# Keys' exponential features in a first stage: fronts two tiles ahead of the sums, sums of features alone for two tiles at a time

## The chip, the cores and the metric

The kernel runs on one core of a Trainium2 chip. The core has TensorE (matrix products, PE in the profile), VectorE (DVE), ScalarE (ACT), GpSimd (POOL) and SyncE (SP, which issues the transfers here). Each works through its own queue in order. The metric is the device time of one execution in microseconds, as the median of several runs.

## The reference

A linear attention feeds two expert layers. The change lies in the attention's keys:

```python
def phi(x):
    proj = np.einsum('bhsd,df->bhsf', x, w_phi)
    proj = proj - np.max(np.abs(proj), axis=-1, keepdims=True)
    return np.concatenate([np.exp(proj), np.exp(-proj)], axis=-1)
q_p, k_p = (phi(q), phi(k))
kv = np.einsum('bhsf,bhsd->bhfd', k_p, v)
z = np.sum(k_p, axis=2)
num = np.einsum('bhsf,bhfd->bhsd', q_p, kv)
den = np.einsum('bhsf,bhf->bhs', q_p, z)[..., None] + 1e-06
return (num / den).astype(np.float32)
```

There are 4 batches, 8 heads, 576 positions, heads of 64 and 128 features, so 256 with both signs. Its result goes, scaled by a root mean square, through a gated layer (512 to 1536 and back), and through a second layer of 8 experts with soft slots.

## The kernel before

**Stages.** Stage one makes the sums kv and z of all four batches, attends the first block of 384 queries, and converts nine of the 18 pieces of the gated layer's weights (each by two passes on ACT, L127 and L129, two on DVE, L137 and L139, a rounding on ACT, L102, and a difference on POOL, L105). Stage two is the gated layer over six blocks (L804, and L829 to L831), with the further queries and weights worked in between. Stage three is the second layer. Stage two begins on TensorE with the first L804.

**A tile of keys.** The 2304 positions make 18 tiles of 128. A tile's *front* is: eight matmuls of the keys with the features (L394, into two buffers P, one for each half hf of the heads), DVE's largest value and its subtraction (L398, L402, into `pr`, three buffers), and ACT's two exponentials (L415, L416, into a buffer `kp` for each half, four in all). A tile's *sums* are eight matmuls of values with features (`kv_of`, L439: 64 columns of the array each, into the accumulators kacc0 for hf 0 and kacc1 for hf 1) and eight of ones with features (`z_of`, L448: 32 columns each, into kacc2). The keys come by L385 (four buffers `raw`), the values by L411 (three).

**Batches.** A batch is 4.5 tiles. Tiles 4 and 13 hold the end of one batch and the start of the next, and their sums are made in two parts; batch 1 ends with tile 8. Where a batch ends, `Evac` copies the accumulators out: kacc0 and kacc2 on ACT (L463), kacc1 on DVE (L461). The accumulators have one buffer each, so the next batch's first sum waits for that copy. The copies are then turned on TensorE (L476) and laid out by L485 and L487.

**The loop over tiles (L519)** issues in turn i: the loads, the front of tile i + 1 up to DVE's subtraction, the sums of tile i, then the exponentials of tile i + 1, with pieces of weight conversion, of turning and of the first block's queries (L322, L325, L326, L337, L339, L206, L214, L216 to L232) between the halves. Ahead of the loop stands the front of tile 0. The order in which each engine gets its instructions is not just this order: a scheduler puts an instruction that it takes for ready ahead of one that it takes for waiting. So runs of matmuls of one line are cut by others.

Of the kernel before, what the change touches and what calls it, by code (L numbers as in the profile page):

```python
# [7 lines left out]
F32 = mybir.dt.float32  # L8
# [8 lines left out]
NB, NH, SEQ, HD, DF = 4, 8, 576, 64, 128  # L17
# [3 lines left out]
TILES = NT // 128  # L21
# [19 lines left out]
def batch_parts(i):  # L41

    t0, parts = i * 128, []
    r = 0
    while r < 128:
        b = (t0 + r) // SEQ
        end = min(128, (b + 1) * SEQ - t0)
        parts.append((b, r, end))
        r = end
    return parts  # L50
# [14 lines left out]
def tile_kernel(ctx: ExitStack, tc: tile.TileContext, q2T, qT, kT, v, wbd, wg, wv, wo, rmsg, phi, w1, w2, consts, out):  # L65
# [3 lines left out]
    def pool(stack, name, space=None, bufs=1, side="left"):  # L69
        kw = {} if space is None else {"space": space}  # L70
        if space is None:
            kw["side"] = side
        if space is not DRAM:
            kw["reuse_waits"] = "tile"
        return stack.enter_context(tc.tile_pool(name=name, bufs=bufs, **kw))
# [73 lines left out]
    def conv_load(sp, bufs, *pools):  # L149

        key = next(conv_at, None)
        if key is not None:
            c = Conv(sp, pools[pieces.index(key) % len(pools)], key, bufs)
            c.load()
            loaded.append(c)

    def conv_scale():
        if loaded:
            convs.append(loaded.pop(0))
            convs[-1].scale()  # L160

    def conv_join():
        if convs:
            convs[-1].join()
            if convs[-1].n == 2:
                joined.append(convs.pop())

    def conv_parts():
        if joined:
            joined.pop(0).parts()  # L170
# [85 lines left out]
    class Reduced(Q):  # L256
# [25 lines left out]
        def exps(self, h):  # L282
            e = self.e[h]
            DVE.tensor_tensor(out=e[:, 1], in0=e[:, 1], in1=e[:, 0], op=ALU.subtract)
            ACT.activation(out=e[:, 0], in_=e[:, 1], func=AF.Exp)
            ACT.activation(out=e[:, 1], in_=e[:, 1], func=AF.Exp, scale=-1.0)
# [83 lines left out]
    with ExitStack() as pk:  # L370
        kx = pool(pk, "kx")
        sp = pool(pk, "spk")
        psk = pool(pk, "psk", PSUM)
        acc = {}

        class Front:

# [30 lines left out]
        class K(Front):  # L408
# [2 lines left out]
                SP.dma_start(out=self.vt, in_=v[self.i].rearrange("p (h d) -> p h d", h=NH))  # L411

            def exps(self, hf):
                kp = sp.tile([128, 4, 2, DF], F32, tag="kp", name="kp", bufs=4)
                ACT.activation(out=kp[:, :, 0], in_=self.pr[hf], func=AF.Exp)  # L415
                ACT.activation(out=kp[:, :, 1], in_=self.pr[hf], func=AF.Exp, scale=-1.0)  # L416
                self.e[hf] = kp

            def kv(self, part):

                for f in (self.kv_of, self.z_of):
                    for hf in range(2):
                        f(hf, part)

            def ends(self, part):
                b, r0, r1 = part
# [66 lines left out]
        ks = [K(sp, psk, kT, i, kb if i else dict(kb, P=("misc", 3))) for i in range(TILES)]  # L493
# [13 lines left out]
        for _ in range(2):  # L507
            conv_load(sp, KCONV, sp)
        conv_scale()
        ks[0].project()  # L510
        for hf in range(2):
            ks[0].shift(hf)
            ks[0].exps(hf)
        fillers = []
        q0 = Turned(sp, psk, 0, {"misc": 3, "raw": 2, "pr": 3, "e": 2})
        qsteps = q0.steps(TURNED0[0:4], TURNED0[4:8], TURNED0[8:])
        qsteps = [[f for m, f in qsteps if m == n] for n in range(2 * TILES)]
        q0.begin()
        for i in range(TILES):  # L519
            k, kn = ks[i], ks[i + 1] if i + 1 < TILES else None  # L520
            if i + 3 < TILES:
                ks[i + 3].load()
            if i + 2 < TILES:
                ks[i + 2].load_v()
            if i % 2 and i // 2 + 2 < NPRE:
                conv_load(sp, KCONV, sp)
            parts = batch_parts(i)
            b = parts[0][0]
            ends = i * 128 + parts[0][2] == (b + 1) * SEQ

            def finish():
                ev = Evac(b)
                fillers.extend([lambda n=n: ev.turn(n) for n in range(3)])

            if len(parts) > 1:
                k.kv(parts[0])
                finish()
            if kn:
                kn.project()
                kn.shift(0)  # L540
                kn.largest(1)
                conv_join()
                kn.less(1)
            k.kv(parts[-1])
            for hf in range(2):
                if kn:
                    kn.exps(hf)
                if hf == 0 and i % 2:
                    conv_parts()
                    conv_scale()  # L550
                if fillers:
                    fillers.pop(0)()
                for f in qsteps[2 * i + hf]:
                    f()
            if ends and len(parts) == 1:
                finish()
# [47 lines left out]
    with ExitStack() as p2:  # L604
# [5 lines left out]
        sp = pool(tctx, "conv")  # L610
# [233 lines left out]
        for blk in range(NBLK):  # L844
            acc = [ps.tile([128, DM], F32, tag=f"acc{i}", name=f"acc{i}", bufs=1) for i in range(TPB)]
            qsteps, qnext = qnext or [], None
            if blk == 1:
# [6 lines left out]
                sp = pool(pctx, "post", side="right")  # L854
            if blk == NBLK - 1:
# [5 lines left out]
                sp = pool(pctx, "post", side="right")  # L861
# [62 lines left out]
    with ExitStack() as p3:  # L924
        sp = pool(p3, "sp3")
# [145 lines left out]
```

## Time and profile before

| what | value |
| --- | --- |
| time, median of 3 runs | 745.16 us (744.03 to 750.23) |
| profiled execution, its time | 744.73 us |
| profiled execution, its span | 742.9 us |
| TensorE busy, whole span | 713.5 us, 96% |
| VectorE, ScalarE busy | 428.1 us, 371.6 us |
| first L804 on TensorE (end of stage one) | 134.23 us |

The busy time of an engine is the time in which an instruction of its was at work; matmuls overlap a little in their records, so that a row's own duration is somewhat longer than the step to the next row. A matmul of this type leaves two records, so "x16" in a row is eight matmuls. In a timeline, a bracket behind a row gives the idle time ahead of it and what ended it.

### The profile page before, as it was taken

The numbers are of one execution on the slowest core, as the hardware profiler recorded it, in microseconds if no ns is written. First come the engines' busy times: TensorE is split into PE (matmuls) and PEld (weight loads), VectorE is DVE, ScalarE is ACT, GpSimd is POOL, SyncE is SP. The second block draws the span as 40 slices with busy tenths as digits, with TensorE's granted clock in tenths as the row PEclk, the third lists the DMA queues.
The fourth block names the chain that finished last, engine by engine and source line by source line (L and its number), as shares of the span: only waits on it lengthen the run. The fifth ranks groups of instructions, "written<-read, shape, count | busy, mean of one in ns | idle before, by whom it ended". The sixth has DMA issues, their size and how long they took to land.

```text
span 742.9 us, 12354 instructions
## 1 busy us (share of the span) xinstructions
PE 713.5 (96%) x4919; PEld 575.1 (77%) x4919; DVE 428.1 (58%) x808; ACT 371.6 (50%) x805; POOL 108.3 (15%) x60
## 2 busy tenths in 40 slices
PE   6999898999899999999999999999999999999894
PEld 4555554888789888898888988889888899988343
DVE  5888956687756646555565555655556453323313
ACT  6689855588644465334654346543465431211103
POOL 0222210135200211012110121101211010000100
PEclk9999999999999999999999999999999999999998
DMA  9674211545010100101000010000100237657898
GB/s 325 225 243 182 72 44 45 187 158 208 8 61 23 33 22 23 49 0 33 22 23 20 1 33 22 23 19 1 33 1 2 65 120 275 228 199 288 318 362 285
DMA packets 25146, 79.47 MB, mean 107 GB/s; under 512 B 2688, under 2 KB 13376, under 8 KB 18688
## 3 DMA queue, kind: packets, MB, share of 16 engines
q1 hardware_dynamic: 24864, 77.79, 30.0%
q10 hardware_dynamic: 224, 0.88, 0.4%
q8 instruction: 39, 0.64, 0.3%
q14 instruction: 19, 0.16, 0.1%
HBM read 71.99 MB, written 6.67 MB: 106 GB/s over the span
## 4 chain that ended last, share of the span: by engine, by line
PE 76%; ACT 10%; DVE 6%; issue 2%; DMA 2%; POOL 1%; SPq 0%; DVEq 0%; ACTq 0%; POOLq 0%
PE pv L804 18%; PE pg L804 17%; PE acc L829 6%; PE acc L830 6%; PE acc L831 6%; PE num L206 4%; PE kacc L439 3%; PE den L214 2%; PE y L943 2%; ACT e L224 2%; PE kacc L448 2%; PE y L959 2%; DVE wt L137 1%; DMA wraw<-in_wg_dram 1%; ACT wt L127 1%
## 5 line engine op out<-in xcount | busy, mean ns | idle before, releaser
L804 PE MATMUL pv<-xnh,wv 128*128 128x384 f32 x576 | 151.6, 344 | 0.0
L804 PE MATMUL pg<-xnh,wg 128*128 128x384 f32 x576 | 150.2, 342 | 1.3 <-DVE t L812 1.0
L804 PEld LDWEIGHTS pg<-xnh,wg 128*128 128x128 f32 x576 | 104.7, 188 | 7.2 <-DVE t L812 1.5
L804 PEld LDWEIGHTS pv<-xnh,wv 128*128 128x128 f32 x576 | 103.2, 188 | 7.0 <-issue 6.7
L804 PE MATMUL pv<-xnl,wv 128*128 128x384 f32 x288 | 97.7, 339 | 0.0
L804 PE MATMUL pg<-xnl,wg 128*128 128x384 f32 x288 | 97.5, 338 | 0.0
L829 PE MATMUL acc<-wo,hh 128*128 128x512 f32 x216 | 88.6, 410 | 0.0
L280 POOL PARTITION_ALL_REDUCE qe<-qe x32 | 50.0, 1563 | 262.7 <-ACT qe L279 243.0
L830 PE MATMUL acc<-wo,hh 128*128 128x512 f32 x216 | 85.9, 397 | 0.0
L831 PE MATMUL acc<-wo,hl 128*128 128x512 f32 x216 | 85.4, 395 | 0.0
L102 ACT CAST hh<-t 128x384 fp32r<-128x384 f32 x72 | 36.7, 509 | 79.8 <-PE acc L830 66.1
L105 DVE TENSOR_TENSOR hl<-t,hh 128x384 fp32r<-128x384 f32 x72 | 41.3, 574 | 52.7 <-ACT hh L102 50.3
L812 DVE SCALAR_TENSOR_TENSOR t<-t,pg 128x384 f32<-128x384 f32 x72 | 39.7, 551 | 51.3 <-ACT t L811 51.2
L811 ACT ACTIVATE t<-pg 128x384 f32<-128x384 f32 x72 | 35.1, 488 | 62.5 <-PE pg L804 62.3
L224 ACT COPY qe<-qe 32x192 f32<-32x192 f32 x128 | 44.8, 350 | 31.7 <-DVE qe L219 30.4
L816 DVE TENSOR_TENSOR t<-t,pv 128x384 f32<-128x384 f32 x72 | 39.8, 552 | 30.2 <-PE pv L804 29.0
L804 PEld LDWEIGHTS pg<-xnl,wg 128*128 128x128 f32 x288 | 54.0, 188 | 0.3 <-DVE xnl L105 0.3
L804 PEld LDWEIGHTS pv<-xnl,wv 128*128 128x128 f32 x288 | 54.1, 188 | 0.1
L439 PE MATMUL kacc<-kp,vt 128*64 128x256 f32 (+1 forms) x320 | 43.8, 399 | 5.3 <-ACT kp L416 5.2
L831 PEld LDWEIGHTS acc<-wo,hl 128*128 128x128 f32 x216 | 40.6, 188 | 10.0 <-DVE hl L105 0.3
L829 PEld LDWEIGHTS acc<-wo,hh 128*128 128x128 f32 x216 | 40.7, 189 | 7.3 <-issue 0.3
L830 PEld LDWEIGHTS acc<-wo,hh 128*128 128x128 f32 x216 | 40.7, 188 | 6.4
(187 smaller groups left out, 1069.2 us busy)
## 6 DMA issues: line engine op xcount, KB each, us to landing
eu<-in_w_dram SPq DMA_DIRECT2D x32, 1024.0 KB, 6.5
wraw<-in_wg_dram SPq DMA_DIRECT2D x6, 1024.0 KB, 5.5
wraw<-in_wv_dram SPq DMA_DIRECT2D x6, 1024.0 KB, 6.6
wraw<-in_wo_dram SPq DMA_DIRECT2D x6, 1024.0 KB, 5.0
qraw<-in_qT_dram SPq DMA_DIRECT2D x32, 192.0 KB, 2.4
raw<-in_kT_dram SPq DMA_DIRECT2D x18, 256.0 KB, 3.5
vt<-in_v_dram SPq DMA_DIRECT2D x18, 256.0 KB, 2.9
out_dram<-ob SPq DMA_DIRECT2D x18, 256.0 KB, 3.4
```

Source lines behind the costliest of these rows:

```text
L102: ACT.copy(out=hi, in_=src)
L105: (lo_eng or POOL).tensor_tensor(out=lo, in0=src, in1=hi.bitcast(F32), op=ALU.subtract)
L224: ACT.copy(out=rd[64 * hh + 32 * r:64 * hh + 32 * r + 32, g], in_=dn[o:o + 32])
L280: POOL.partition_all_reduce(e[:, 0], e[:, 1], channels=128, reduce_op=bass_isa.ReduceOp.absmax)
L439: PE.matmul(out=kva[o0:o0 + 64, hh // 2], lhsT=self.vt[r0:r1, h], rhs=kp[r0:r1, hh].rearrange("p s f -> p (s f)"), start=first and hh < 2, ...
L804: PE.matmul(out=p, lhsT=w[:, a, c], rhs=x, start=n == 0, stop=n == 11)
L811: ACT.activation(out=t, in_=g, func=AF.Tanh, scale=0.5)
L812: DVE.scalar_tensor_tensor(out=t, in0=t, scalar=1.0, in1=g, op0=ALU.add, op1=ALU.mult)
L816: DVE.tensor_tensor(out=t, in0=t, in1=wide("v", m, xs), op=ALU.mult)
L829: PE.matmul(out=acc[i], lhsT=hh[:, s], rhs=w[:, 0], start=m == 0, stop=False)
L830: PE.matmul(out=acc[i], lhsT=hh[:, s], rhs=w[:, 1], start=False, stop=False)
L831: PE.matmul(out=acc[i], lhsT=hl[:, s], rhs=w[:, 0], start=False, stop=m == MF - 1)
```

## The change

Three edits in stage one. The `kp` buffers go from four to eight. In `kv`, a tile's matmuls of L439 are issued at once, but those of L448 are kept in a list and issued for two tiles together, or where a batch ends. The fronts are two tiles ahead: tiles 0 and 1 are projected, shifted and exponentiated before the loop, turn i works the front of tile i + 2, and the keys' loads are one tile further ahead.

```diff
--- before.py
+++ after.py
@@ -371,7 +371,7 @@
         kx = pool(pk, "kx")
         sp = pool(pk, "spk")
         psk = pool(pk, "psk", PSUM)
-        acc = {}
+        acc, zs = {}, []
 
         class Front:
 
@@ -411,16 +411,21 @@
                 SP.dma_start(out=self.vt, in_=v[self.i].rearrange("p (h d) -> p h d", h=NH))
 
             def exps(self, hf):
-                kp = sp.tile([128, 4, 2, DF], F32, tag="kp", name="kp", bufs=4)
+                kp = sp.tile([128, 4, 2, DF], F32, tag="kp", name="kp", bufs=8)
                 ACT.activation(out=kp[:, :, 0], in_=self.pr[hf], func=AF.Exp)
                 ACT.activation(out=kp[:, :, 1], in_=self.pr[hf], func=AF.Exp, scale=-1.0)
                 self.e[hf] = kp
 
             def kv(self, part):
 
-                for f in (self.kv_of, self.z_of):
-                    for hf in range(2):
-                        f(hf, part)
+                for hf in range(2):
+                    self.kv_of(hf, part)
+                zs.append((self, part))
+                if len(zs) == 2 or self.ends(part)[1]:
+                    for k, p in zs:
+                        for hf in range(2):
+                            k.z_of(hf, p)
+                    zs.clear()
 
             def ends(self, part):
                 b, r0, r1 = part
@@ -507,19 +512,21 @@
         for _ in range(2):
             conv_load(sp, KCONV, sp)
         conv_scale()
-        ks[0].project()
-        for hf in range(2):
-            ks[0].shift(hf)
-            ks[0].exps(hf)
+        ks[3].load()
+        for k in ks[0:2]:
+            k.project()
+            for hf in range(2):
+                k.shift(hf)
+                k.exps(hf)
         fillers = []
         q0 = Turned(sp, psk, 0, {"misc": 3, "raw": 2, "pr": 3, "e": 2})
         qsteps = q0.steps(TURNED0[0:4], TURNED0[4:8], TURNED0[8:])
         qsteps = [[f for m, f in qsteps if m == n] for n in range(2 * TILES)]
         q0.begin()
         for i in range(TILES):
-            k, kn = ks[i], ks[i + 1] if i + 1 < TILES else None
-            if i + 3 < TILES:
-                ks[i + 3].load()
+            k, kn = ks[i], ks[i + 2] if i + 2 < TILES else None
+            if i + 4 < TILES:
+                ks[i + 4].load()
             if i + 2 < TILES:
                 ks[i + 2].load_v()
             if i % 2 and i // 2 + 2 < NPRE:
```

What becomes of the order on the engines is seen at three places. First, TensorE's queue just behind the first two fronts; kacc_166 and kacc_192 are batch 0's kacc0, kacc_167 and kacc_193 its kacc1, kacc_168 and kacc_194 its kacc2. Before:

```order
L394 MATMUL P<-wbd_f,raw 128x128 x16
L439 MATMUL kacc_166<-kp,vt 64x256 x4
L448 MATMUL kacc_168<-kp,small 32x256
L439 MATMUL kacc_167<-kp,vt 64x256 x4
L448 MATMUL kacc_168<-kp,small 32x256 x7
L394 MATMUL P<-wbd_f,raw 128x128 x8
```

After:

```order
L394 MATMUL P<-wbd_f,raw 128x128 x16
L444 MATMUL kacc_192<-kp,vt 64x256 x4
L453 MATMUL kacc_194<-kp,small 32x256
L444 MATMUL kacc_193<-kp,vt 64x256
L394 MATMUL P<-wbd_f,raw 128x128 x8
L444 MATMUL kacc_193<-kp,vt 64x256 x3
L444 MATMUL kacc_192<-kp,vt 64x256 x4
L453 MATMUL kacc_194<-kp,small 32x256 x8
```

Both begin with two tiles' fronts. The third front moves into the first tile's sums, and the runs of L448 (L453 after) are cut once more here; over the stage they are 27 runs before and 14 after.

Second, TensorE at the joint of batches 1 and 2, that is of tiles 8 and 9, with buffer numbers: kp_765 and kp_780 are the two halves of tile 9 before, kp_700 and kp_715 after; kp_791 and kp_806 are those of tile 10 after. Before:

```order
L439 MATMUL kacc0_820<-kp_765,vt_635 64x256 x4
L439 MATMUL kacc1_821<-kp_780,vt_635 64x256 x4
L448 MATMUL kacc2_822<-kp_765,small_77 32x256 x4
L448 MATMUL kacc2_822<-kp_780,small_77 32x256 x4
L476 MATMUL kvt_848<-cst_72,kvs0_788 128x128 x4
```

After:

```order
L444 MATMUL kacc1_847<-kp_715,vt_653 64x256 x4
L444 MATMUL kacc1_847<-kp_806,vt_754 64x256 x4
L444 MATMUL kacc0_846<-kp_700,vt_653 64x256 x4
L481 MATMUL kvt_866<-cst_72,kvs0_814 128x128 x4
L337 MATMUL T_873<-cst_72,qpr_803 128x128 x2
```

The sums into kacc1 of two tiles now come first, the second of them with tile 10's features, and the first sum into kacc0 stands behind them; tile 9's L453 come later, with tile 10's.

Third, ACT at the same joint; kvs0_788 is the copy out of batch 1's kacc0 before, kvs0_814 after. Before:

```order
L224 COPY e2_532<-e2_532 32x192 x8
L415 ACTIVATE kp_765<-pr_742 128x4x128
L416 ACTIVATE kp_765<-pr_742 128x4x128
L463 COPY kvs0_788<-kacc0_424 128x512
L231 ACTIVATE e2_532<-xraw_596 128x384
```

After:

```order
L102 CAST wg2_1170<-wt_1027 128x1024
L129 ACTIVATE wraw_992<-wraw_992 128x1024
L129 ACTIVATE wraw_1112<-wraw_1112 128x1024
L224 COPY e2_558<-e2_558 32x192 x8
L415 ACTIVATE kp_791<-pr_768 128x4x128
L416 ACTIVATE kp_791<-pr_768 128x4x128
L339 ACTIVATE e2_794<-T_795 128x2x128
L231 ACTIVATE e2_558<-xraw_614 128x384
L339 ACTIVATE e2_794<-T_795 128x2x128
L415 ACTIVATE kp_806<-pr_773 128x4x128
L416 ACTIVATE kp_806<-pr_773 128x4x128
L468 COPY kvs0_814<-kacc0_450 128x512
```

Counted from the start of the queue, 19 pairs L415, L416 stand ahead of that copy before and 22 after, and with them one L127, two L129, one L102, four L339 and one L231 more.

## Rows read from the trace of the kernel before

**Rows 1.** Stretches: length, busy us of PE, PEld, DVE, ACT, POOL; granted clock; DMA

```profile
0.00:134.20 134.20, 120.58 (x1130) 69.97 (x1130) 97.84 (x165) 97.69 (x188) 22.45 (x13) 0.99 0.46 157
50.00:95.00 45.00, 40.90 (x408) 23.19 (x405) 39.51 (x62) 41.08 (x86) 12.31 (x6) 1.00 0.40 140
95.00:134.20 39.20, 36.52 (x345) 20.35 (x344) 22.64 (x50) 20.54 (x46) 2.31 (x1) 0.96 0.14 42
118.00:119.00 1.00, 1.00 (x8) 0.56 (x6) 1.00 (x5) 0.00 (x0) 0.00 (x0) 0.50 0.00 0
134.20:160.00 25.80, 25.77 (x159) 23.39 (x159) 19.55 (x28) 17.61 (x28) 5.71 (x3) 1.00 0.58 199
```

**Rows 2.** TensorE's groups by line, 71.3 to 134.3 us: busy, mean ns | idle before

```profile
L439 PE MATMUL kacc<-kp,vt 128*64 128x256 f32 (+1 forms) x160 | 22.0, 409 | 3.9 <-ACT kp L416 3.8
...
L394 PE MATMUL P<-wbd_f,raw 64*128 64x128 f32 x114 | 11.4, 289 | 0.6 <-DVE pr L402 0.5
```

**Rows 3.** TensorE's timeline: start us, duration us, instruction, records [idle before <-releaser]

```profile
4.60 3.78 PE L394 MATMUL P<-wbd_f,raw 64*128 64x128 f32 x32 [4.60 <-DMA raw<-in_kT_dram]
...
10.82 0.62 PE L448 MATMUL kacc<-kp,small 128*32 128x256 f32 x2
11.37 1.08 PE L439 MATMUL kacc<-kp,vt 128*64 128x256 f32 x8
12.38 1.06 PE L448 MATMUL kacc<-kp,small 128*32 128x256 f32 x14
13.38 1.16 PE L394 MATMUL P<-wbd_f,raw 64*128 64x128 f32 x16
```

**Rows 4.** TensorE's timeline, eight sums of a tile, and batch 2's first

```profile
65.38 1.95 PE L439 MATMUL kacc<-kp,vt 128*64 128x256 f32 x16
...
71.37 1.08 PE L439 MATMUL kacc<-kp,vt 128*64 128x256 f32 x8
```

**Rows 5.** TensorE's timeline, a run of one front

```profile
98.34 0.48 PE L394 MATMUL P<-wbd_f,raw 64*128 64x128 f32 x2
```

**Rows 6.** ACT's timeline from the copy out of batch 1's kacc0

```profile
70.05 0.57 ACT L463 COPY kvs<-kacc 128x512 f32<-128x512 f32 x1
70.52 0.53 ACT L231 ACTIVATE e<-xraw 128x384 f32<-128x384 f32 x1
70.94 0.65 ACT L339 ACTIVATE e<-T 128x256 f32<-128x256 f32 x2
71.47 0.64 ACT L415 ACTIVATE kp<-pr 128x512 f32<-128x512 f32 x1
...
72.51 0.67 ACT L339 ACTIVATE e<-T 128x256 f32<-128x256 f32 x2
...
73.50 1.22 ACT L127 ACTIVATE wt<-wraw 128x1024 f32<-128x1024 f32 x1
74.57 2.29 ACT L129 ACTIVATE wraw<-wraw 128x1024 uint32<-128x1024 uint32 x2
```

**Rows 7.** TensorE's timeline to the end of the first stage

```profile
117.09 3.34 PE L439 MATMUL kacc<-kp,vt 128*64 128x256 f32 x16
...
128.47 1.08 PE L439 MATMUL kacc<-kp,vt 128*64 128x256 f32 x8 [1.79 <-ACT kp L416]
...
134.23 0.62 PE L804 MATMUL pg<-xnh,wg 128*128 128x384 f32 x2 [0.23 <-ACT xnh L102]
```

**Rows 8.** ACT's timeline, its five longer gaps ahead of that copy

```profile
23.34 0.63 ACT L415 ACTIVATE kp<-pr 128x512 f32<-128x512 f32 x1 [2.47 <-DVE pr L402]
...
25.89 1.04 ACT L339 ACTIVATE e<-T 128x256 f32<-128x256 f32 x3 [1.40 <-PE T L337]
...
36.20 1.04 ACT L102 CAST wo<-wt 128x1024 fp32r<-128x1024 f32 x1 [1.51 <-DVE wt L139]
...
47.80 0.17 ACT L487 COPY kv<-kvt 128x8 f32<-128x8 f32 x1 [0.88 <-PE kvt L476]
...
52.28 1.20 ACT L127 ACTIVATE wt<-wraw 128x1024 f32<-128x1024 f32 x1 [1.07 <-POOL wg L105]
```

## The prediction

> **What bounds the kernel now.** I read the busy times by stretch first [rows 1]. Up to 134.2 us, where the matmuls of the expert layer begin, TensorE is busy 120.6 us; DVE and ACT are busy 97.8 and 97.7 us of the same stretch. In the first 25.8 us behind it TensorE is busy 25.77 us. So the later stages are TensorE's, nothing in them is touched, and a stage one that ends x us earlier ends the kernel x us earlier. The question is only where in stage one TensorE loses time. The groups by line for 71.3 to 134.3 us [rows 2] name it: of TensorE's idle time there 3.8 us stand ahead of L439 (the sums of keys by values) waiting for ACT's exponentials, and 0.5 us ahead of L394 waiting for DVE. The largest of the 3.8 is 1.79 us at the last tile [rows 7].
>
> The other loss is not idle time. Four matmuls of L448 fill the four column strips of the array together, two of L439 the two halves. A run of 7 L448 matmuls takes 1.00 us (12.38 to 13.38), a single one 0.55 us (10.82 to 11.37) [rows 3]: two rounds against one, so a round is 0.45 us and starting a run 0.10. Four of L439 take 1.01 us to the next row, 0.07 less than their own 1.08, eight so 1.95 less 0.07, 1.88 [rows 3, 4]: a round of two is 0.435, a start 0.14. Eight matmuls of a front (L394) take by the same reckoning 1.09 us, one 0.41 [rows 3, 5]: about 0.31 + 0.097 n. (A matmul is two records in the trace.) Splitting runs costs starts and half-filled rounds: one L448 matmul and then seven cost 1.55 us, where eight together cost about 1.0.
>
> **The change, part by part.** *Amounts.* Every engine issues the same instructions; loads are as many and as large. On SP raw 3 passes the first two q loads, and raw i+4 replaces raw i+3; behind the first tile no row of TensorE waits for a transfer [rows 2, 3], so I cost the moved transfers at nothing, covered by four raw buffers. The first two fronts already stood ahead of the first sums on TensorE, so the start and its wait stay.
>
> *Runs.* I count what stands on TensorE from the joint of the second and third batch, where batch 2's first sum into kacc0 begins at 71.37 [rows 4], to the end of the stage. Before, L448 there is 2 runs of 1, 2 of 4, 2 of 7 and 7 of 8: 1.1 + 1.1 + 2.0 + 7.0 = 11.2 us. After, 4 of 16 and 2 of 8. A run of 16 is not in the trace: at most 2.00 (two of 8), at least four rounds and no start, 1.80; I take 1.90. That is 9.6, so 1.6 less. Fronts: 12 runs with 56 matmuls before (9.2 us by the formula), 7 with 48 after (6.8), because one tile's front now lies ahead of the joint: 2.4 less. L439: 6 runs of 4 and 7 of 8 before, 19.2; after, eight of its matmuls lie ahead of the joint, and the rest is 38 rounds with 10 starts, 17.9: 1.3 less. Together 5.3 us.
>
> *Waits.* With fronts a tile earlier a tile's exponentials are done before its sums are due: all 3.8 us of [rows 2] go, if ACT keeps up. Late in the stage it does: from 95 to 134.2 us ACT is busy 20.5 of 39.2 us [rows 1].
>
> *What the change puts in the way.* At the joint, kacc0 must first be copied out by ACT (L463). That copy is issued behind the exponentials of the tile whose front is made in the same turn, and this is now two tiles ahead. Before, it starts at 70.05 [rows 6]. After, ACT has this more ahead of it: three pairs L415, L416 at 1.04 (71.47 to 72.51) = 3.1; one L127 at 1.07 (73.50 to 74.57); two L129, 2.2; one L102, 1.0; four L339 at 0.53 for two = 1.1; L231 0.4 [rows 6, 8]. Sum 8.9. ACT idled, ahead of the copy, in five longer gaps of 2.47, 1.40, 1.51, 0.88 and 1.07 us [rows 8], 7.3 in all. Fronts a tile earlier fill the first, which waits for DVE's shifted keys, and the fourth, a wait for sums turned on TensorE, ahead of which a tile's exponentials now stand ready. The second waits for q's transposes, the third for a conversion on DVE that runs long, the fifth for POOL; nothing in the change touches those. So 3.35 us come back: the copy starts at 70.05 + 8.9 - 3.35 = 75.6 and ends 0.5 later, 76.1. TensorE would be there at about 73.3 (71.4, where it now arrives, and 1.9 for eight kacc1 matmuls that now go first). It waits, and all behind it on its queue wait too: the next front, the next runs of L448, and through that front DVE.
>
> *Sum.* From the joint to the end of the stage it takes 134.23 - 71.37 = 62.9 us now [rows 4, 7]. After: 62.9 - 5.3 - 3.8 = 53.8. The stage ends at 76.1 + 53.8 = 129.9, where it now ends at 134.2: 4.3 us earlier. The profiled execution takes 744.73 us (span 742.9 and 1.83 around it), so 740.4; the median shown is 745.16, 0.4 above, which I leave inside the range.
>
> *Bounds of the unknown.* If no gap of ACT closes, the copy ends at 79.5, the stage at 133.3, and the time is 743.8. If all 7.3 us close, the copy ends at 72.1, before TensorE comes; the stage ends at 73.3 + 53.8 = 127.1, and the time is 737.6. A run of 16 at 2.00 or 1.80 moves this by 0.4 either way.
>
> *The clock.* Rows show half clock once within the stage: 0.50 in 118 to 119 us [rows 1], 1.2 GHz of 2.4, where eight L439 matmuls take 3.27 us in place of 1.88 [rows 4, 7]. No wait for ACT or DVE ahead of it since 71.3 us is as long as the 1.79 us of the last tile, behind which four matmuls of L439 take their usual 1.08 us [rows 2, 7]. At the very start, after 4.6 us without work, two tiles' fronts take 3.78 us where two times 1.09 would do, 1.6 more, though the record there says full clock [rows 3]. The wait at the joint (2.8 us by the sum) lies between those gaps, so I leave it at full speed, with 1.6 us as the price if not. The Trainium skill, page "TensorE: Matmul & The Clock Gate", section "Why this matters for your kernels", speaks against the change here: a long idle gap between bursts of matmuls sends the engine back to half clock. By that rule the wait at the joint would be paid twice, and the sum would be 740.4 + 1.6 = 742.0; the stretch at 118 us, at half clock with hardly a gap ahead of it, is not explained by that rule alone.
>
> **The rivals.**
> A. *The copy is not late.* ACT closes its gaps, since a tile of exponentials always waits for it. Then the stage is TensorE's own sum: 737.6, or 736.2 if the half-clock stretch at 118 us (1.4) goes as well. For it: TensorE waited for ACT most just where ACT was full, so small leads may help more than gap by gap. Against: three of five gaps have causes outside the fronts.
> B. *ACT gains nothing.* The prefetched exponentials only move ACT's idle time. Copy ends at 79.5: 743.8, no change by measurement. For it: ACT is busy 41.1 and DVE 39.5 of the 45 us from 50 to 95 us [rows 1], and DVE's waits on ACT for shifted keys stay, with three buffers for them.
> C. *Slower.* The same late copy leaves TensorE idle for 6.2 us (73.3 to 79.5), and the clock falls: 1.6 more, 745.4, slower by 0.7. It decides once the copy ends after 76.1 + 4.3 = 80.4 at full clock, or after 78.8 at half. For it: it is the longest gap the order can make, longer than the one at the start. Against: DVE and q's buffers hold TensorE back on the way, so that the gap is spread.
>
> **How the numbers follow.** About 1% (7.4 us) is what a measurement of this kernel tells from no change. The forecast (copy late by 1 to 5 us, with or without the clock's 1.6; 738.5 to 742.5) has 0.5; A 0.25, with its half at the clock's end under 737.3 us; B 0.15; C 0.1, half of it for a joint so much worse than its price here that it costs over a per cent. The predicted time is the forecast's, 740.4. The range 736.0 to 745.5 reaches from A's end to C; outside lie about 0.05 below and 0.07 above, and the spread of the runs. Faster by over 1%: 0.18, from A and a little of the forecast's end; slower: 0.06; within: 0.76.
>
> **What would show it.** Right: L439's idle time for L416 behind 72 us under 0.5 us; L448 in runs of 32 records of about 1.9 us; the ACT copy out of batch 1's kacc0 starting near 75.6 us, and TensorE idle ahead of batch 2's first kacc0 sum by two to three microseconds; L804 starting near 130 us; the same length behind it. Wrong: that copy at 72 (A) or 79 (B); the granted clock at 0.5 just after the joint (C); or a length behind the stage that differs by over 1 us, which would mean that moved tiles reach into stage two, for which I saw no sign in the order.

## The result and the profile after

The changed kernel takes 739.48 us (median of 12 runs, 737.16 to 743.2), beside 745.36 us of the kernel before on the same chip: a ratio of 0.992 (95% interval 0.990 to 0.9935). Measured twice more it gave 739.28 us (0.992, 0.989 to 0.994) and 738.01 us (0.990, 0.987 to 0.992). So 740.4 was forecast and 738 to 739.5 came out: less time than before by somewhat under one per cent, as the likeliest case said.

Three executions of the changed kernel were profiled. The first one is among the longest of its twelve runs (742.41 us), so it is not enough by itself. This is TensorE's timeline of it (start us, duration us, instruction, records, and in brackets the idle time ahead and what ended it), from the wait ahead of the joint of batches 1 and 2 to the end of stage one:

```profile
67.49 0.70 PE L322 MATMUL P<-wbd_f,qraw 128*128 128x256 f32 x2 [1.33 <-ACT xraw L216]
...
74.20 1.08 PE L444 MATMUL kacc<-kp,vt 128*64 128x256 f32 x8
77.52 2.11 PE L444 MATMUL kacc<-kp,vt 128*64 128x256 f32 x16 [2.23 <-ACT kp L416]
...
82.90 1.93 PE L453 MATMUL kacc<-kp,small 128*32 128x256 f32 x32
...
130.54 0.61 PE L811 MATMUL pg<-xnh,wg 128*128 128x384 f32 x2 [0.23 <-ACT xnh L102]
```

Stage one ends at 130.54 us, where it ended at 134.23 [rows 7]. Behind the wait at 77.5 us no sum of keys by values waits for exponentials any more; here are TensorE's groups by line for 77.5 to 130.6 us of the same profile (busy us, mean ns, idle ahead), to be read beside [rows 2]:

```profile
L444 PE MATMUL kacc<-kp,vt 128*64 128x256 f32 (+1 forms) x152 | 19.8, 386 | 2.2 <-ACT kp L416 2.2
L453 PE MATMUL kacc<-kp,small 128*32 128x256 f32 (+1 forms) x160 | 10.0, 383 | 0.0
L394 PE MATMUL P<-wbd_f,raw 64*128 64x128 f32 x96 | 8.1, 284 | 0.4 <-PE T L337 0.4
```

The 2.2 us left ahead of L444 is the wait at the joint. ACT's timeline there (first profile) shows the copies out of batch 1's sums, which answer to L463 in [rows 6]:

```profile
76.32 0.63 ACT L415 ACTIVATE kp<-pr 128x512 f32<-128x512 f32 x1
76.84 0.62 ACT L416 ACTIVATE kp<-pr 128x512 f32<-128x512 f32 x1
77.36 0.66 ACT L339 ACTIVATE e<-T 128x256 f32<-128x256 f32 x2
77.89 1.09 ACT L468 COPY kvs<-kacc 128x512 f32<-128x512 f32 x2
```

The second profile (the control run of the experiments) is 5.2 us shorter, in TensorE's and then ACT's timeline:

```profile
65.34 0.70 PE L322 MATMUL P<-wbd_f,qraw 128*128 128x256 f32 x2 [2.11 <-ACT xraw L216]
65.97 2.08 PE L394 MATMUL P<-wbd_f,raw 64*128 64x128 f32 x16
67.98 2.61 PE L444 MATMUL kacc<-kp,vt 128*64 128x256 f32 x16
...
75.31 2.11 PE L444 MATMUL kacc<-kp,vt 128*64 128x256 f32 x16 [0.59 <-ACT kp L416]
...
128.33 0.61 PE L811 MATMUL pg<-xnh,wg 128*128 128x384 f32 x2 [0.23 <-ACT xnh L102]
```

```profile
74.64 0.62 ACT L416 ACTIVATE kp<-pr 128x512 f32<-128x512 f32 x1
...
75.68 1.09 ACT L468 COPY kvs<-kacc 128x512 f32<-128x512 f32 x2
```

The third agrees with the second to 0.02 us at these rows, but for the two between 65.9 and 68.5 us, which come 0.47 us later in it. What separates the profiles most is where TensorE ran at half clock (1.2 of 2.4 GHz); all three, like the kernel before, also have it in their last 4 to 6 us. Stretches of the first (length, busy us of PE, PEld, DVE, ACT and POOL, granted clock, DMA share and rate):

```profile
51.80:55.20 3.40, 3.40 (x21) 2.23 (x19) 3.10 (x7) 3.26 (x7) 0.63 (x1) 0.50 0.36 101
690.00:697.00 7.00, 6.47 (x32) 2.97 (x36) 2.71 (x15) 0.46 (x2) 0.00 (x0) 0.51 0.59 211
```

Cut at three rows that all kernels have (the first matmul of stage two, the first L722 or L729 of the last block's router, and the last L980 or L987), a profiled execution reads, in us, worked out from the starts of those rows:

| profile | stage one ends | half clock in stage one | to the router | router to last combination | rest | span |
| --- | --- | --- | --- | --- | --- | --- |
| before | 134.23 | 117.5 to 121 | 554.0 | 43.8 | 10.8 | 742.9 |
| changed, first | 130.54 | 51.8 to 55.2 | 552.9 | 46.8 | 10.3 | 740.5 |
| changed, second | 128.33 | 66 to 69.4 | 552.9 | 43.8 | 10.3 | 735.3 |
| changed, third | 128.33 | 65.4 to 68.8 | 552.8 | 43.7 | 11.3 | 736.2 |

So stage one gained 3.7 or 5.9 us. Behind it the first profile loses 3.0 us to the half clock at 690 to 697 us, which the other two do not have; and the kernel before spent about 1 us more in stage two in its profile than any other kernel here. The granted clock, which each run lists as a mean, fits this: three of the twelve runs have 0.989, as the first profile, and take 742.3 to 742.5 us, and eight have 0.993 to 0.995 and take 737.2 to 740.0 us. The longest run (743.2 us at 0.995) is not explained by the clock.

### The profile page after: what moved, and what is told of

Same layout as the page of the kernel before. It is cut to its first block, busy times and chain, and to the rows that moved or that the text cites. A ratio compares the mean times of both kernels' runs of the same rounds, so it can differ in the third digit from the quotient of the medians.

```text
span 740.5 us, 12341 instructions
## 1 busy us (share of the span) xinstructions
PE 710.9 (96%) x4919; PEld 576.2 (78%) x4919; DVE 430.9 (58%) x808; ACT 371.2 (50%) x805; POOL 107.9 (15%) x60
## 4 chain that ended last, share of the span: by engine, by line
PE 77%; ACT 9%; DVE 6%; DMA 3%; issue 2%; POOL 1%; SPq 1%; DVEq 0%; POOLq 0%; ACTq 0%
PE pv L811 19%; PE pg L811 18%; PE acc L836 6%; PE acc L837 6%; PE acc L838 6%; PE num L206 4%; PE kacc L444 2%; PE y L950 2%; PE den L214 2%; DMA wraw<-in_wg_dram 2%; PE y L966 2%; ACT wt L127 2%; ACT e L224 1%; DVE wt L137 1%; PE P L394 1%
## 5 line engine op out<-in xcount | busy, mean ns | idle before, releaser
L102 ACT CAST hh<-t 128x384 fp32r<-128x384 f32 x72 | 36.7, 510 | 80.7 <-PE acc L837 66.1
L105 DVE TENSOR_TENSOR hl<-t,hh 128x384 fp32r<-128x384 f32 x72 | 41.3, 574 | 51.2 <-ACT hh L102 48.6
L819 DVE SCALAR_TENSOR_TENSOR t<-t,pg 128x384 f32<-128x384 f32 x72 | 39.7, 551 | 51.6 <-ACT t L818 51.6
L224 ACT COPY qe<-qe 32x192 f32<-32x192 f32 x128 | 44.8, 350 | 31.7 <-DVE qe L219 30.4
L444 PE MATMUL kacc<-kp,vt 128*64 128x256 f32 (+1 forms) x320 | 44.4, 395 | 4.1 <-ACT kp L416 4.1
```

The costliest lines, as they stand in the source:

```text
L102: ACT.copy(out=hi, in_=src)
L105: (lo_eng or POOL).tensor_tensor(out=lo, in0=src, in1=hi.bitcast(F32), op=ALU.subtract)
L224: ACT.copy(out=rd[64 * hh + 32 * r:64 * hh + 32 * r + 32, g], in_=dn[o:o + 32])
L444: PE.matmul(out=kva[o0:o0 + 64, hh // 2], lhsT=self.vt[r0:r1, h], rhs=kp[r0:r1, hh].rearrange("p s f -> p (s f)"), start=first and hh < 2, ...
L819: DVE.scalar_tensor_tensor(out=t, in0=t, scalar=1.0, in1=g, op0=ALU.add, op1=ALU.mult)
```

## The experiments

Each kernel ran in five rounds beside the kernel before. In the diffs the lines are those of the changed kernel unless it is said otherwise.

**Sums of features for two tiles, alone** (the kernel before, with the list `zs` and eight buffers; the fronts stay one tile ahead):

```diff
-                for f in (self.kv_of, self.z_of):
-                    for hf in range(2):
-                        f(hf, part)
+                for hf in range(2):
+                    self.kv_of(hf, part)
+                zs.append((self, part))
...
```

> One part alone: the sums of features wait for two tiles and take them together, with eight feature buffers; the keys' fronts stay one tile ahead, as before. Theory (the fronts ahead carry the gain): behind the joint of batches 1 and 2 the runs of the sums of features are 16, 1, 15, 8, 16, 1, 15, 1 and 7 matmuls in the issue order, 11.2 us by the formula of the prediction against 11.2 before, so the pairing saves nothing by itself, and the waits of L444 for ACT's exponentials (3.8 us behind 71 us, 1.79 of it at the last tile) stay: within 1 us of the kernel before, 744 to 746 us. Rival (the pairing carries it): the longer runs give back 2 us or more by themselves and push the sums behind the exponentials, 741 to 743 us.

Measured: 746.51 us, ratio 1.000 (0.998 to 1.0015). In time the theory holds: the kernel with pairing alone is no faster. TensorE's timeline shows waits for exponentials that stay: the one at the joint is there without the fronts ahead, and longer, and the last tile still waits (0.89 us, where it was 1.79 in [rows 7]).

```profile
74.22 3.68 PE L444 MATMUL kacc<-kp,vt 128*64 128x256 f32 x16 [3.26 <-ACT kp L416]
...
128.86 1.08 PE L444 MATMUL kacc<-kp,vt 128*64 128x256 f32 x8 [0.89 <-ACT kp L416]
```

The clock was not the same, though. Eleven of its twelve runs have a granted clock of 0.990 or less, where most runs of the kernel before have 0.995, and in its profile TensorE is at half clock for 10.2 us of stage one (49.5 to 53.0 and 73.4 to 80.3 us, the second from within the wait at the joint on) and again at 694.7 to 701.5 us; stage one still ends at 134.63 us. The one run at 0.993 took 742.68 us, less than any run of the kernel before. So pairing may save something that the clock takes back; no run here separates the two.

**Fronts two tiles ahead, alone** (the changed kernel with the sums of features behind each tile):

```diff
-                for hf in range(2):
-                    self.kv_of(hf, part)
-                zs.append((self, part))
...
+                for f in (self.kv_of, self.z_of):
+                    for hf in range(2):
+                        f(hf, part)
```

> The other part alone: keys' fronts two tiles ahead and eight feature buffers; the sums of features follow each tile's sums, as before. Theory (the fronts ahead carry the gain): behind the joint there are ten runs of eight in place of four of 16 and two of 8, 10.0 us against 9.6, and as much again ahead of the joint, and no wait of L439 for L416 behind the joint: about 0.8 us slower than the changed kernel (739.5), 740.3 us. Rival (the pairing carries it): the time goes back to within 1 us of the kernel before, 744.5 to 746 us.

Measured: 740.92 us, ratio 0.993 (0.990 to 0.995). In time the fronts carry nearly all of the gain; the pairing on top of them is worth some 0.8 us by the ratios, the size expected, though the intervals overlap. In its profile no L439 waits for L416 behind the first tile. But the split is one of times at the clock that each kernel happened to get: this profile is at half clock from 66.9 to 73.7 us, with a wait of 2.90 us for L216 there, and from 118.1 to 121.5 us, and its stage one ends at 132.59 us, 1.6 us earlier than before, where the changed kernel gained 3.7 or 5.9. What each part is worth within stage one stays open.

**Eight buffers alone** (the kernel before):

```diff
-                kp = sp.tile([128, 4, 2, DF], F32, tag="kp", name="kp", bufs=4)
+                kp = sp.tile([128, 4, 2, DF], F32, tag="kp", name="kp", bufs=8)
```

> The buffers alone: the kernel before with eight feature buffers in place of four; the issue order is that of before on TensorE and ACT. Theory: no row of ACT waits for a feature buffer to come free in the kernel before, its exponentials wait for DVE's shifted keys, so the time stays at 745.4 us, within 0.5 us. Rival (buffers were short): exponentials start earlier, the 3.8 us of L439's waits shrink, 742 to 744 us.

Measured: 747.14 us, ratio 1.0005 (0.999 to 1.002): nothing, as expected. Its profile has half clock behind the router (693.5 to 700.3 us), which that of the kernel before has not; stage one ends at 133.79 us, 0.4 us earlier, with the waits of before in their places:

```profile
77.49 1.08 PE L439 MATMUL kacc<-kp,vt 128*64 128x256 f32 x8 [0.79 <-ACT kp L416]
79.35 1.08 PE L439 MATMUL kacc<-kp,vt 128*64 128x256 f32 x8 [0.77 <-ACT kp L416]
...
128.02 1.08 PE L439 MATMUL kacc<-kp,vt 128*64 128x256 f32 x8 [1.74 <-ACT kp L416]
```

**The copies ahead of the exponentials:**

```diff
             k.kv(parts[-1])
+            ev = Evac(b) if ends and len(parts) == 1 else None
             for hf in range(2):
...
-            if ends and len(parts) == 1:
-                finish()
+            if ev:
+                fillers.extend([lambda n=n, ev=ev: ev.turn(n) for n in range(3)])
```

> The changed kernel with one line moved: where a batch ends with a whole tile (between batches 1 and 2, and at the last), the copies out of its sums are issued ahead of the turn's exponentials, not behind them. Theory (the wait of 2.2 us at 77.5 us in the changed kernel is for ACT's copy out of kacc0, which stands behind exponentials of a tile that nobody needs yet): ACT's copy L468 starts near 72 us, TensorE's wait ahead of batch 2's first sum into kacc0 is under 0.5 us, and about 2 us come off 739.5: 737.5 us. Rival (the wait only moves: the exponentials behind the copy are late for the sums that now come earlier, or a copy out of kvt is): 739.5 us, and a wait of about 2 us ahead of L444 or L206 between 73 and 95 us.

Measured: 743.72 us, ratio 0.997 (0.995 to 0.998): slower than the changed kernel, by 3.7 us if one goes by the ratios. My theory falls in its second half. The copy does start at 72.12 us and no L444 waits at the joint; but TensorE then stops further on, ahead of a front:

```profile
65.36 1.20 PE L322 MATMUL P<-wbd_f,qraw 128*128 128x256 f32 x2 [2.23 <-ACT xraw L216]
...
92.79 1.13 PE L394 MATMUL P<-wbd_f,raw 64*128 64x128 f32 x8 [1.58 <-issue]
...
129.06 0.61 PE L812 MATMUL pg<-xnh,wg 128*128 128x384 f32 x2 [0.23 <-ACT xnh L102]
```

The trace names no releaser at 92.79, but a front needs a buffer P that DVE's L402 has read, and DVE's timeline has that instruction ending at 92.68, behind a sum that waited for ACT's eight copies L224:

```profile
91.53 0.56 DVE L225 TENSOR_TENSOR xraw<-xraw,e 128x384 f32<-128x384 f32 x1 [1.15 <-ACT e L224]
92.00 0.68 DVE L402 TENSOR_TENSOR pr<-P,mx 128x512 f32<-128x512 f32 x1
```

In the changed kernel the same L402 starts at 91.27 us, and the front at 92.06 with 0.41 us of waiting. So DVE and ACT come to this place no earlier with the earlier copy, and what TensorE gains at the joint it waits for there. With half clock at the same place (65 us) stage one ends 0.7 us later than in the second profile of the changed kernel, not 2 us earlier. More lies behind stage one: half clock from 686.6 to 696.9 us, and 47.9 us from the router to the last combination where 43.8 do. This profile was the fastest of its twelve runs, and their granted clock is mostly 0.987, lower than the 0.989 to 0.995 of the changed kernel. Beside the second profile of the changed kernel, 4.1 of this one's 4.9 us more of span lie behind the router, with the clock, and 0.7 in stage one, so the moved wait is the smaller part of the loss; where the other runs lost more is not seen in a trace.

**The changed kernel again:**

> The changed kernel again, beside the next three. If its runs fall where they fell first: 0.992 of the kernel before, some 739.5 us, with about a third of the runs near 742.4. What separates those in the profile is a stretch at half clock (1.2 GHz) from 690.1 to 696.9 us, where the router of the last block leaves TensorE waits of 0.2 to 0.6 us; in it the first 32 records of the expert sums take 5.84 us and not 3.64.

Measured: 739.28 us, ratio 0.992 (0.989 to 0.994), two of the six runs at 741.6 and 742.2. It is the second profile above. In the first profile, with half clock behind the router, the first expert sums take 5.84 us, in this one, without it, 3.64:

```profile
692.45 5.84 PE L950 MATMUL y<-eu,xo 128*32 128x512 f32 x32 [0.44 <-DVE xo L777]
```

```profile
689.41 3.64 PE L950 MATMUL y<-eu,xo 128*32 128x512 f32 x32 [0.43 <-DVE xo L777]
```

**Three matmuls more in the router of the last block:**

```diff
                 t2(2)
+                s = ps.tile([96, DM], F32, tag="gv", name="sps", bufs=2)
...
+                        PE.matmul(out=s[0:32], lhsT=phi_sb[:, 0], rhs=x2[0].rearrange("p c t -> p (c t)"), start=True, stop=True)
+                warm(2)
...
+                warm(1)
```

> The changed kernel with three matmuls more that nobody reads (128x512, two records each, into the bank that the router's sums of rows take next), issued in the router of the last block between the logits and the turned minimum, where TensorE waits 0.46 and 0.62 us. Theory (the stretch at half clock behind the router follows from TensorE's thin work in it, and costs 2 to 3 us in the runs that have it): the stretch at 690 us is gone from all or nearly all runs, the first 32 records of the expert sums take 3.64 us, the runs near 742.4 are missing, and the three matmuls cost at most 0.5 us: 738 to 739.5 us. Rival (the clock falls there whatever TensorE does, by something outside this stretch): as many slow expert sums as in the run beside it, 739.5 to 740.5 us.

Measured: 741.99 us, ratio 0.994 (0.992 to 0.996), 2.7 us more than the changed kernel beside it. All seven runs have a granted clock of 0.993 or more, and the profile has no half clock behind the router:

```profile
692.10 3.64 PE L957 MATMUL y<-eu,xo 128*32 128x512 f32 x32 [0.15 <-DVE xo L784]
```

This fits the theory that thin work there is what the clock fell on, but does not prove it: 17 of the 24 runs of the changed kernel are above 0.991 too, so that seven of seven would come by chance about once in eleven times, and six of the seven, at 0.993 and 1.3 to 1.6 us longer than the profiled run at 0.995, have room for another short stretch that no trace shows. And the price was not the 0.5 us that I gave: from the router to the last combination it takes 45.5 us, 1.7 more than undisturbed. Of these, 1.0 lie ahead of the expert sums (9.19 us behind the router's first row, where the second profile of the changed kernel has 8.18). That is more than the stretch costs on average (3.0 us, in about a third of the runs). It does not explain all of the 2.7 us: in this profile stage one ends at 130.04 us, with half clock from 51.7 us on, as in the first profile of the changed kernel.

**The same three matmuls in the kernel with the earlier copies:**

```diff
+                warm(2)
...
+                warm(1)
```

> The kernel with ACT's copies ahead of the exponentials (743.7 us, though its first stage ended at 129.06 us, 1.5 us before the changed kernel's) with the same three matmuls more. Theory (what the earlier copy gains in stage one is lost behind the router, where that kernel's profile shows half clock from 686.4 to 696.6 us): the stretch is shorter or gone, and the time falls to 737 to 739 us, 1 to 2 us below the changed kernel with the three matmuls. Rival (the copy's loss comes from elsewhere): 742 to 744 us, with stage one ending later than 130 us in its profile.

Measured: 743.66 us, ratio 0.9975 (0.9955 to 0.9994). No gain, and the rival's numbers hold: the profile has half clock twice in stage one, from 65.6 to 69 us and, behind the wait of 1.58 us at 92.4 us, from 92.9 to 96.3 us, and the stage ends at 130.33 us. So part of what the earlier copy loses lies in stage one. The stretch behind the router became shorter (693.6 to 697 us) but did not go, so that this run says nothing on what the kernel would take without it.

**All other work of a turn ahead of the exponentials** (the kernel with the earlier copies):

```diff
             for hf in range(2):
-                if kn:
-                    kn.exps(hf)
...
                 for f in qsteps[2 * i + hf]:
                     f()
...
+                if kn:
+                    kn.exps(hf)
```

> The kernel with ACT's copies ahead of the exponentials, and now all other work of a turn (q's attention, the turned sums, the weights' conversion) issued ahead of the turn's exponentials too. Theory (TensorE's wait of 2.23 us at 65.4 us for ACT's copy L216, 1.33 in the changed kernel, is for exponentials that nobody needs yet, and the half clock from 65.6 to 69 us follows it): wait under 1 us, stage one ends by 128 us, and the time goes down by about 1 to 2 us against the same kernel without (743.7): 741.5 to 742.7 us. Rival (the exponentials then come too late for the sums): waits of L444 for L416 of 1 us or more behind 60 us, stage one not earlier than 129 us.

Measured: 741.29 us, ratio 0.993 (0.991 to 0.996). The time is just below the theory's range, but the mechanism is not there: the wait for L216, now at 64.3 us, is 2.23 as before, the one at 92 us (now at 91.4) is longer, TensorE then ran at half clock from 92.9 to 99.8 us, and stage one ended at 130.88 us:

```profile
91.42 1.13 PE L394 MATMUL P<-wbd_f,raw 64*128 64x128 f32 x8 [2.01 <-issue]
92.48 2.40 PE L444 MATMUL kacc<-kp,vt 128*64 128x256 f32 x10
```

The scheduler still put two pairs of exponentials ahead of L216 on ACT, so the edit did not do there what it was meant to, and where its gain of 2.4 us over the kernel with the earlier copies comes from is open. What the second profile of the changed kernel shows at this place is a shortage: the second L322 wants one of three PSUM buffers, which the first projection (read by DVE's L326 until 65.8 us), num (copied by L216 until 65.3 us) and den hold. The next two runs keep them apart.

**The second attention of block 0 two turns later:**

```diff
-TURNED0 = [2, 8, 14, 20, 12, 15, 20, 26, 28, 31]
+TURNED0 = [2, 8, 14, 20, 12, 17, 20, 26, 28, 31]
```

> The changed kernel with one number of q's table of turns changed: the second pair of heads of block 0 attends in turn 17 and not 15, so that its sums (num, den) no longer stand between two of q's projections (L322) that need the same three PSUM buffers. Theory (TensorE's wait of 1.3 to 2.1 us at 65 to 67 us for ACT's copy L216 out of num, and the half clock that follows it in some profiles, are the next loss of stage one after the change): that wait is under 0.5 us, no half clock at 65 to 69 us, stage one ends at 126 to 128 us (128.33 and 130.54 in the two profiles of the changed kernel), 737 to 738 us. Rival (the wait moves with the attention, to the copies and transposes at the joint): a wait of 1.5 us or more for L216, L468 or L416 between 68 and 80 us, 739 to 741 us.

Measured: 740.61 us, ratio 0.993 (0.990 to 0.995). The wait for L216 at 65 us is gone and no half clock stands there, but there is one at 51.6 to 55.0 us, and stage one ends at 129.81 us, later than the theory's 126 to 128. The rival came true in place and size: a wait of 1.71 us stands with the attention, though for the turned queries' exponentials (L339) and none of the three that I had named.

```profile
72.12 0.86 PE L214 MATMUL den<-e,kv 128*32 128x192 f32 x16 [1.71 <-ACT e L339]
```

**The second and third attention away from all projections:**

```diff
-TURNED0 = [2, 8, 14, 20, 12, 15, 20, 26, 28, 31]
+TURNED0 = [2, 8, 14, 20, 12, 19, 23, 26, 28, 31]
```

> As the last, with the second pair of heads in turn 19 and the third in turn 23 (not 15 and 20): no attention of block 0 then stands in a turn with q's projections. Theory: neither the wait at 65 us nor the one at 92 us (ahead of L394, behind DVE's L225 that waits for ACT's eight copies L224; 0.4 us in the changed kernel, 1.6 to 2.0 with the copies ahead of the exponentials) is left, stage one ends at 126 to 128 us, 737 to 738 us. Rival (the later attention runs late at the end of the stage: attend of the fourth pair, scale and output follow, and the first rows of the expert layer wait for them): waits ahead of L241 or L811 of 2 us or more, 740 to 743 us.

Measured: 737.63 us, ratio 0.989 (0.986 to 0.991). The waits at 65 us and for L402 at 92 us are gone (0.2 and 0.8 us stand at 69.6 and 75.7, 1.2 us at 90.7), and stage one ends 1.5 us ahead of the changed kernel's best:

```profile
69.57 1.13 PE L394 MATMUL P<-wbd_f,raw 64*128 64x128 f32 x14 [0.19 <-DVE pr L402]
...
75.67 1.51 PE L206 MATMUL num<-e,kv 128*64 128x384 f32 x8 [0.80 <-ACT e L339]
...
90.66 0.86 PE L214 MATMUL den<-e,kv 128*32 128x192 f32 x16 [1.20 <-ACT e L339]
...
126.88 0.62 PE L811 MATMUL pg<-xnh,wg 128*128 128x384 f32 x2 [0.23 <-ACT xnh L102]
```

It was run once more, now beside the changed kernel on one chip:

> The kernel with the attention of block 0 in turns 19 and 23 once more, now on the same chip as the changed kernel (next). Theory (its first stage ends 1.5 to 3.7 us earlier, 126.9 against 128.3 and 130.5): 736.5 to 738 us, 1.5 to 3 us below the changed kernel. Rival (the first comparison was of different chips): within 1 us of the changed kernel.

> The changed kernel, the measure for the run before this one: 739 to 740 us, 0.992 of the kernel before. Its profile is a third sample of where the half clock falls in stage one: if at 51 us, the wait ahead of batch 2's sums (77.5 us) is near 2.2 and the stage ends near 130.5 us; if at 65 us, near 0.6 and 128.3.

Measured: 735.95 us, ratio 0.986 (0.983 to 0.988), and 738.01 us, ratio 0.990 (0.987 to 0.992), both below what was expected. By medians the moved attention is worth 2.1 us on top of the change; the two intervals overlap a little. Its profile has no half clock in stage one, which ends at 126.66 us, but has it behind the router (686.2 to 693.0 us). By its median it is the fastest kernel of this study. The third profile of the changed kernel has half clock at 65.4 us, a wait of 0.61 us at 75.30 and the stage's end at 128.33 us, as was expected for that place.

## Why the prediction was right, and where it was lucky

**The bound.** Stage one's TensorE was rightly taken as what the end follows: 552.8 to 553.2 us lie between the end of stage one and the router in all thirteen profiles taken behind the prediction, whatever was done in stage one. The 554.0 of the kernel before was the exception, so the sum was made against a profile with 1.1 us that were its own (some of them show as one wait of stage two, L804 for DVE's L812: 1.0 us, in the later profiles 0.2 to 0.6).

**Runs.** A run of 16 L453 matmuls was priced at 1.90 us; its records take 1.93, and 1.87 to the next row (82.90 to 84.77 us). Right. From the joint on L453 is busy 10.0 us where it was 12.4, L394 8.1 where it was 11.4, L444 19.8 where it was 22.0: 7.9 less against 5.3 forecast. 1.4 of the difference is the half clock of [rows 7], which has gone from there. These are busy times of two windows that do not begin at the same sum; by starts (below) the runs gave about 1.0 more than forecast.

**Waits for exponentials.** All 3.8 us of [rows 2] went. Right, but two smaller waits that were not there before came behind them in all three profiles: 0.52 us for DVE's L232 and 0.22 us for L246.

**The copy at the joint.** Forecast for 75.6 us; 75.68 in two profiles, 77.89 in the third. Right to 0.1 us in those two. In the first profile it comes 2.2 us later, and that begins ahead of the half clock: ACT waited in it for transfers of weights, 0.85 us at 13.05 us and 0.97 us at 39.89 us,

```profile
39.89 1.16 ACT L129 ACTIVATE wraw<-wraw 128x1024 uint32<-128x1024 uint32 x1 [0.97 <-DMA wraw<-in_wv_dram]
```

and TensorE is 1.3 us behind the second profile at 51.0 us (L337 at 51.01 and 49.70). The half clock from 51.8 us on then makes num late, for which ACT waits 1.59 us. The prediction put the moved transfers at nothing, since no row of TensorE waits for one. But ACT waits for transfers of weights in all eleven profiles of kernels with the fronts two tiles ahead (0.2 to 1.8 us in all), and in none of the three with the fronts one tile ahead. Whether the keys' transfers, moved forward on the same queue, delay them, or ACT comes to them earlier, no run separates.

**The wait at the joint.** Forecast 2.8 us; 2.23, 0.59 and 0.61. The place is right. What ends it is not the copy: TensorE's order, shown ahead of the prediction, has tile 10's sum into kacc1 in front, and that waits for tile 10's exponentials, the last work ahead of the copy on ACT but for two L339; the copy itself is done when TensorE comes to kacc0. And TensorE comes later than the forecast 73.3: at 74.7 and 75.3 us, because it had waited 1.3 to 2.1 us for L216 at 65 to 67 us and, in the second and third profiles, then ran at half clock. That wait was not among the terms: before, TensorE stood there for 0.88 us, and for DVE:

```profile
63.69 0.67 PE L322 MATMUL P<-wbd_f,qraw 128*128 128x256 f32 x2 [0.88 <-DVE qpr L326]
```

**The sum.** Stage one was to end at 129.9 us; 130.54, 128.33, 128.33. The term that was off is from the joint to the end: 53.8 us forecast from the first sum into kacc0. That sum starts about 1.0 us (four matmuls and a start, as in [rows 3]) behind 77.52 and 75.31, and from there 52.0 us are left in each. Of the 1.8 us, 1.4 are the half clock at 118 us, which I had left in for the forecast and taken out only in rival A; the other 0.4 are runs, about 1.0 better than priced, less some 0.6 of new waits.

**The clock.** Left at full speed at the joint: right in all three profiles, in the first behind 2.23 us without work. Half clock came instead at 51.8 us (behind 1.28 us of waiting for L339) or at 65 us (behind 2.1 us for L216). Its price of 1.6 us was right by luck, since it was read from the start of the kernel, where the granted clock is 1.00 from 4.6 to 8.4 us: in the second profile the front and the sums at 65.97 and 67.98 us take 2.08 and 2.61 us, where 1.16 and 1.95 are usual. The Trainium skill's rule that I had weighed (page "TensorE: Matmul & The Clock Gate", section "Why this matters for your kernels": a long idle gap sends the engine back to half clock) fits eight of the twelve waits of 2 us or more that the thirteen later profiles have in stage one behind the first tile, and not the other four, of which two stand at this joint; and in the kernel before half clock began behind a wait of half a microsecond, so the rule alone does not tell where it falls.

**Same length behind the stage.** Wrong in two of three profiles by more than the 1 us that I had set as a mark: 608.7 before, 610.0, 607.0 and 607.9 after. No moved tile reaches into stage two; it is the 1.1 us of the kernel before and the 3.0 us of half clock behind the router. These have opposite signs, and the median of the changed kernel lies between its profiles; that 739.5 came so near 740.4 owes something to it.

**The rivals.** A's time (737.6, or 736.2) is near that of the second profile (738.10), but its mechanism did not come: the copy was late as forecast, stage one ended at 128.33 us and not at A's 127.1, and the time came so low through the clock, the runs and the 1.1 us of stage two, not through ACT. B and C have nothing for them: ACT's gaps did close where the fronts were to fill them. Of the five of [rows 8] the second profile has two left ahead of the copy, 2.02 us for TensorE's transposes and 1.40 us for POOL; the first profile has these and three new ones (0.85 and 0.97 us for weights' transfers, 1.59 us for num).

## What to carry to other kernels

Prefetching one stage of a chain further ahead removes the waits on it at once, but the engine in the middle then works on what nobody needs yet, and the next wait stands at the first thing that queues behind that. Before moving a late instruction ahead, look at which engine sets the pace over the next 20 us: here an earlier copy moved TensorE's wait to DVE, while two numbers in a table that kept two users of three PSUM buffers apart gave about 2 us by the medians. Where the parts of a change are tried alone, compare the granted clocks of their runs before their times are set against each other. And where the effect is under 1%, cut several profiles at common rows before believing one span.

## What the runs showed of the hardware that I had not expected

The half clock decides nearly as much as the change does: of the 24 runs of the changed kernel those at a granted clock of 0.995 took 736.4 to 738.3 us (but for one of 743.2), those at 0.989 took 741.4 to 742.5. Behind the router TensorE has small matmuls and waits of 0.2 to 0.6 us, and half clock followed in nine of the thirteen later profiles, 3.4 to 10.2 us of it; where no matmuls were added, the way from the router to the last combination then takes 46.6 to 47.9 us and not 43.8. It comes and goes between executions of one kernel; what makes one kernel have it in nearly all runs (eight buffers alone: granted clock 0.990 or less in eleven of twelve) and another in a third is not settled. For one place the record shows what goes with it: in the kernels with the fronts two tiles ahead, half clock at 51.6 to 52.2 us stands in just those four profiles in which ACT waited 0.4 us or more (0.97, 1.10, 0.43 and 0.80) for weights at 39 to 40 us. Half clock ahead of a wait can cost little: in the second profile it makes 2.61 us at 67.98 us of a group that takes 1.95 us ([rows 4]), but TensorE then still waits 0.59 us at the joint for exponentials of ACT, which is never idle for more than 0.1 us from 59.5 to 81.9 us.

DVE's conversion step L139 takes 1.21 us alone (77.27 us, second profile) and 2.69 us at 82.76 us, while POOL's L105 runs from 82.00 to 84.37 us; the next L402 starts at its end.
